# Loads of a retention block and of a gated MLP: by head over 128 partitions, k and all of w_in on GpSimd's queue

## The chip, the cores and the metric

The kernel runs on one core of a Trainium2 chip. The core has a matrix engine (TensorE, PE in the profile, with its weight loads PEld beside it), VectorE (DVE), ScalarE (ACT), GpSimd (POOL) and SyncE (SP), which here only issues transfers. Each engine works through its own instructions in order and waits for others by semaphores. Transfers between memory and the core's SBUF are issued by SP, ACT or POOL on queues of their own and are carried out by 16 DMA engines that all queues share. Matrix products land in PSUM, from where DVE or ACT copy them. The metric is the device time of one execution in microseconds, the median over the runs shown.

## The reference

q, k and v have 8 batches, 8 heads, 576 rows and 64 columns. The first part is causal attention with a decay per head and no softmax:

```python
scores = scale * np.matmul(q, k.transpose(0, 1, 3, 2))
gamma = 1.0 - 2.0 ** (-5.0 - np.arange(H, dtype=np.float32))
rel = pos[:, None] - pos[None, :]
Dmat = np.where(rel >= 0, gamma[:, None, None] ** rel[None, :, :], 0.0)
ret = scores * Dmat[None, :, :, :]
return np.matmul(ret, v).astype(np.float32)
```

Its output is laid out as 4608 tokens of 512 columns. The second part is an MLP on the tokens:

```python
h = x @ w_in                       # 512 -> 2048
sp = np.where(h > 20.0, h, np.log1p(np.exp(np.minimum(h, 20.0))))
g = h * np.tanh(sp)                # Mish
return (g @ w_out).astype(np.float32)   # 2048 -> 512
```

All inputs and the output are float32.

## The kernel before

The 576 rows of a batch are cut into chunks of 128 rows (the last 64 rows of two batches share one). Four chunks make a tile of 512 tokens; there are nine tiles. Tiles 0 and 1 hold the first chunk of each of the eight batches, which need no state from earlier rows. Later chunks add a state: the sum of k times v over the earlier rows of the batch, kept with the decay folded into q and v.

Each tile goes through attention, then `g1` (16 groups of four matmuls with w_in, each followed by Mish on ACT), then `g2` (64 matmuls with w_out) and the stores. The order of instructions on every engine is written out by hand: `manual_schedule` keeps the order of the program, so an instruction that waits holds up all that stands behind it on its engine. PE's order decides most: from tile 1 on, the steps of the next tile's attention are slipped between the groups of `g1` and `g2`.

Tiles 0 and 1 have an attention of their own, `f_...` in the code. `load_first` (L97) brings q and k of a tile with 16 loads of 128 KB on SP, each for one batch and four heads, into 32 partitions of `stage`: partition 32b+g holds four successive rows 4g to 4g+3 of batch b. `f_cast` (L176) turns a pair of heads into bf16 and sorts by the row within the four. `f_transpose` (L184) transposes 128x128 blocks (two heads by 64 columns) for each of the four rows, first q's four and then k's four, and after each four a copy brings them from PSUM to SBUF, back in the order of rows. For tile 0 q's and k's transposes have a PSUM tile each; for tile 1 they share one. `f_scores` (L199) makes the scores of a pair of heads and multiplies them on DVE with the decay mask. `f_v` (L211) casts v, `f_out` (L216) makes the output of one batch and copies it to xT; in tile 1 two batches share a PSUM tile. `f_state` (L234) scales v on POOL for the states, and `f_k` (L240) copies the cast k from SBUF to SBUF on SP into the layout that `state` (L314) reads.

v of tile 0 and the first 512 columns of w_in come on SP too (L109, L116); the latter are cast by DVE (L446). The other three quarters of w_in and all of w_out come on POOL's queue, which casts on the way; then v of tile 1 and the chunks from 8 on, three loads each (`load`, L248). After that POOL alternates between loads and the product vs (`step_v`, L271). The buffers for v (`vraw`) are five: a load waits until the product and the cast that read the buffer before are done.

Before g2 of tile 0 (`g2_first`, L385) is run in 16 steps, `first_steps` (L464) says ahead of which step a transposition or a score of tile 1 stands. `keep_warm` issues idle matmuls early on. The result buffers of `store` (L408) are three, so the fourth copy waits for the first store.

Of the kernel before, what the change touches and what calls it, by code (L numbers as in the profile page):

```python
# [10 lines left out]
F32 = mybir.dt.float32  # L11
BF16 = mybir.dt.bfloat16
AX = mybir.ActivationFunctionType
# [4 lines left out]
def kernel(  # L18
# [26 lines left out]
    KC = d_model // P  # L45
# [18 lines left out]
    first = ctx.enter_context(tc.tile_pool(name="first", bufs=1))  # L64
    io = ctx.enter_context(tc.tile_pool(name="io", bufs=PF))
# [6 lines left out]
    ps_sc = ctx.enter_context(tc.tile_pool(name="ps_sc", bufs=2, space=PS))  # L72
# [7 lines left out]
    w_in_t = wpool.tile([P, KC, d_ff], BF16)  # L80
# [1 line left out]
    w_in_r = moe_w_in.rearrange("(c p) f -> p c f", p=P)  # L82
    w_out_r = moe_w_out.rearrange("(f p) d -> p f d", p=P)

    def load_w_in(i):
        nc.gpsimd.dma_start(out=w_in_t[:, :, ts(i, 512)], in_=w_in_r[:, :, ts(i, 512)])

    def load_w_out(i):
        nc.gpsimd.dma_start(out=w_out_t[:, ts(i, 4), :], in_=w_out_r[:, ts(i, 4), :])
# [1 line left out]


    stage = gp.tile([P, 2, H, 4 * D], F32, name="gT")
    qf, kf = stage[:, 0], stage[:, 1]
    v0 = {}

    def load_first(t):  # L97
        for half in range(2):
            hs = ds(4 * half, 4)
            for dst, src in ((qf, q), (kf, k)):  # L100
                for b in range(4):
                    nc.sync.dma_start(  # L102
                        out=dst[ds(32 * b, 32), hs, :],
                        in_=src[4 * t + b, hs, 0:P, :].rearrange("h (g r) d -> g h (r d)", r=4))

    def load_first_v(t):
        for b in range(4 * t, 4 * t + 4):
            v0[b] = io.tile([P, H, D], F32, name="vraw")
            (nc.gpsimd if t else nc.sync).dma_start(out=v0[b], in_=v[b, :, 0:P, :].rearrange("h p d -> p h d"))  # L109

    load_first(0)
    load_first_v(0)
    w0 = []
    for c in range(KC):
        w0.append(io.tile([P, 512], F32, name="qraw"))
        nc.sync.dma_start(out=w0[c], in_=w_in_r[:, c, 0:512])  # L116

    zeros = consts.tile([P, 512], BF16)
    nc.vector.memset(zeros, 0.0)
    ident = consts.tile([P, P], BF16)  # L120
# [23 lines left out]
    nc.scalar.activation(gq, ex, AX.Exp)  # L144
    nc.scalar.activation(gv, ex, AX.Exp, scale=-1.0)
    warm = consts.tile([P, 1], F32)
    nc.scalar.activation(warm, pos[:, 0:1], AX.Mish)
    nc.vector.tensor_scalar(gq, gq, 1.0 / math.sqrt(D), None, op0=OP.mult)

    diag = consts.tile([P, 2], F32)  # L150
# [21 lines left out]
    k0 = {}  # L172
    v0s = {}
    fst = {}

    def f_cast(t, p, which, copy):  # L176
        if p == 0 and which == 0:
            fst[t] = {"qb": first.tile([P, 4, H, D], BF16, name="qb"),
                      "kb": first.tile([P, 4, H, D], BF16, name="kb", bufs=2), "vb": {}}
        name, src = (("qb", qf), ("kb", kf))[which]  # L180
        copy(fst[t][name][:, :, ds(2 * p, 2), :],
             src[:, ds(2 * p, 2), :].rearrange("p h (r d) -> p r h d", r=4))

    def f_transpose(t, p, copies):  # L184
        if t == 0:
            tps = [ps_h.tile([P, 4, P], BF16, name="hp") for _ in range(2)]
        else:
            both = ps_sc.tile([P, 2, 8, P], BF16, name="sc")
            tps = [both[:, i, 0:4] for i in range(2)]
        for i, name in enumerate(("qb", "kb")):  # L190
            out_t = first.tile([P, 4, P], BF16, name=name + "T", bufs=2)
            for r in range(4):
                nc.tensor.transpose(tps[i][:, r, :],
                                    fst[t][name][:, r, ds(2 * p, 2), :].rearrange("p h d -> p (h d)"), ident)
            copies[i](out_t.rearrange("p b (g r) -> p b g r", r=4),
                      tps[i].rearrange("p r (b g) -> p b g r", b=4))
            fst[t][name, p] = out_t

    def f_scores(t, p):  # L199
        qT, kT = fst[t]["qb", p], fst[t]["kb", p]  # L200
        sc = ps_sc.tile([P, 2, 4, P], F32, name="sc")
        for b in range(4):
            for e in range(2):
                r = ds(64 * e, 64)
                nc.tensor.matmul(sc[:, e, b, :], lhsT=kT[r, b, :], rhs=qT[r, b, :], start=True, stop=True)  # L205
        sm = first.tile([P, 2, 4, P], BF16, name="sm0", bufs=4)
        nc.vector.tensor_tensor(sm, sc, dmask[:, ds(2 * p, 2), :].unsqueeze(2).to_broadcast([P, 2, 4, P]),  # L207
                                op=OP.mult)
        fst[t]["sm", p] = sm

    def f_v(t, b, copy):  # L211
        vb = first.tile([P, H, D], BF16, name="vb", bufs=4)
        copy(vb, v0[4 * t + b])
        fst[t]["vb"][b] = vb

    def f_out(t, b, copy):  # L216
        if b == 0:
            xts[t] = xp.tile([P, KC, NCH * P], BF16, name="xT")
        vb = fst[t]["vb"][b]
        if t == 0:  # L220
            pool, name = ((ps_st, "st"), (ps_o, "ops"))[b % 2]
            ot = pool.tile([P, NP, P], F32, name=name)
        else:
            if b % 2 == 0:
                fst[t]["ot"] = ps_sc.tile([P, 2, NP, P], F32, name="sc")
            ot = fst[t]["ot"][:, b % 2]
        for p in range(NP):
            for e in range(2):
                nc.tensor.matmul(ot[ds(64 * e, 64), p, :], lhsT=vb[:, 2 * p + e, :],
                                 rhs=fst[t]["sm", p][:, e, b, :],  # L230
                                 start=(p == 0), stop=True, skip_group_check=True)
        copy(xts[t][:, :, ts(b, P)], ot)  # L232

    def f_state(t, b):  # L234

        n = 4 * t + b
        v0s[n] = first.tile([P, H, D], BF16, name="v0s", bufs=B)
        nc.gpsimd.tensor_tensor(v0s[n], v0[n], gv[:, 0, :].unsqueeze(2).to_broadcast([P, H, D]), op=OP.mult)

    def f_k(t, b):  # L240
        n = 4 * t + b
        k0[n] = first.tile([P, H, D], BF16, name="k0", bufs=B)
        nc.sync.dma_start(out=k0[n].rearrange("p h d -> p (h d)"),
                          in_=fst[t]["kb"][ds(32 * b, 32)].rearrange("p r h d -> p r (h d)"))

# [178 lines left out]
    dve, act, pool = nc.vector.tensor_copy, nc.scalar.copy, nc.gpsimd.tensor_copy  # L424


    for p in range(NP):
        f_cast(0, p, 0, pool if p % 2 else dve)
        f_cast(0, p, 1, pool)
    load_first(1)  # L430
    keep_warm(8)
    for p in range(NP + 1):
        if p < NP:
            f_transpose(0, p, (act, act))
            keep_warm(2)
        if p > 0:
            f_scores(0, p - 1)
    f_v(0, 0, pool)
    f_v(0, 1, act)
    f_v(0, 2, pool)  # L440
    f_v(0, 3, act)
    for i in range(1, 4):
        load_w_in(i)
    for b in range(4):
        f_out(0, b, (dve, act)[b % 2])
        dve(w_in_t[:, b, 0:512], w0[b])  # L446
    for b in range(4):
        f_state(0, b)
        f_k(0, b)
    for i in range(4):  # L450
        load_w_out(i)
    load_first_v(1)
    make_masks()


    for p in range(NP):
        f_cast(1, p, 0, dve)
        f_cast(1, p, 1, dve)
    for f in range(nF):
        g1(0, f)  # L460
    for b in range(4):
        f_k(1, b)
    load(N0)
    first_steps = {0: (f_transpose, 0), 1: (f_transpose, 1), 3: (f_scores, 0), 4: (f_scores, 1),  # L464
                   6: (f_transpose, 2), 7: (f_transpose, 3), 9: (f_scores, 2), 11: (f_scores, 3)}
    for i in range(nF):
        if i in first_steps:
            step, p = first_steps[i]
# [114 lines left out]
```

## Time and profile before

| | us |
|---|---|
| median of 3 runs | 334.22 (334.13 to 334.87) |
| the profiled execution | 335.18 |
| its span | 333.5 |
| PE busy | 309.7 (93%) |
| ACT busy | 137.6 (41%) |
| POOL busy | 136.0 (41%) |
| DVE busy | 117.2 (35%) |

The times in the profile are from the start of the span. A group's idle time is that of the engine ahead of it, with the instruction or transfer that ended it behind an arrow. In the timeline a row merges like instructions; the number of them follows the x. POOL's DMA rows are the time in which it writes a load's descriptors; when the load lands is told by another view. Matmul ends are modelled, so the last 0.2 us of a group can overlap the next. The granted clock is 1.00 at full speed and 0.50 at half.

### The profile page before, as it was taken

The page shows a single profiled execution, that of the slowest core. Times are in us where ns is not written, and L with a number is a line of the kernel's source. Part 1 is how long each engine was busy: PE and PEld are TensorE (multiplying, and loading weights), DVE is VectorE, ACT ScalarE, POOL GpSimd, SP SyncE. Part 2 cuts the span into 40 slices and gives each one's busy share as a digit, 9 for nine tenths or more (in the row PEclk, how much of TensorE's full clock was granted, in tenths as well). Part 3 has the DMA queues.
Part 4 walks back from the last instruction along what each step waited for, and adds up shares of the span by engine and source line. Part 5 has one row for each costly group of instructions (what it writes and reads, how often), then busy time and mean ns, then how long its engine had stood idle before and what let it go on. Part 6 is the DMA issues. An engine that isn't in the chain of part 4 may idle for free.

```text
span 333.5 us, 5849 instructions
## 1 busy us (share of the span) xinstructions
PE 309.7 (93%) x2400; PEld 151.5 (45%) x2400; DVE 117.2 (35%) x162; ACT 137.6 (41%) x252; POOL 136.0 (41%) x167
## 2 busy tenths in 40 slices
PE   5839788699999999999999999999999999999996
PEld 1514344335544554545445454545454544444444
DVE  2481243435533524242525152525252522000111
ACT  6526511367626653534343534334344432333300
POOL 2495325699939295444455353626310000000000
PEclk9969999879999999999999999999999999999999
DMA  7999998998889599979495959697450500010022
GB/s 176 214 268 244 241 244 153 244 170 146 156 171 165 113 128 166 148 157 191 96 191 104 184 109 176 113 173 126 82 126 15 115 31 33 31 31 33 31 79 78
DMA packets 74841, 45.46 MB, mean 136 GB/s; under 512 B 57024, under 2 KB 65984, under 8 KB 74816
## 3 DMA queue, kind: packets, MB, share of 16 engines
q0 software_dynamic: 37808, 23.08, 44.2%
q1 hardware_dynamic: 36864, 21.90, 29.8%
q8 instruction: 18, 0.29, 0.4%
q10 hardware_dynamic: 144, 0.13, 0.1%
q14 instruction: 7, 0.06, 0.1%
HBM read 36.70 MB, written 9.44 MB: 138 GB/s over the span
## 4 chain that ended last, share of the span: by engine, by line
PE 81%; DMA 9%; SPq 3%; DVE 2%; ACT 2%; issue 1%; DVEq 0%; ACTq 0%
PE hp L365 34%; PE ops L380 30%; DMA gT<-in_k_dram 6%; PE st L328 3%; PE sc L296 2%; PE hp L380 2%; PE hp L391 2%; DMA qraw<-in_moe_w_in_dram 2%; ACT ssb L332 2%; SPq L102 1%; DMA gT<-in_q_dram 1%; PE sc L346 1%; SPq L109 1%; PE hp L402 1%; PE sc L283 1%
## 5 line engine op out<-in xcount | busy, mean ns | idle before, releaser
L365 PE MATMUL hp<-xT,w_in_t 128*128 128x512 bf16 x576 | 147.6, 386 | 4.3 <-DVE xT L232 3.2
L367 ACT ACTIVATE gT<-hp 128x512 bf16<-128x512 f32 x144 | 86.1, 598 | 126.1 <-PE hp L365 124.6
L380 PE MATMUL ops<-w_out_t,gT 128*128 128x512 bf16 x464 | 117.9, 379 | 0.3 <-DVE res L410 0.3
L365 PEld LDWEIGHTS <-w_in_t 128*128 128x128 bf16 x576 | 53.8, 99 | 67.5 <-issue 4.0
L380 PEld LDWEIGHTS <-gT 128*128 128x128 bf16 x496 | 48.3, 98 | 58.4 <-issue 1.0
L410 DVE COPY res<-ops 128x512 f32<-128x512 f32 x30 | 20.7, 691 | 144.3 <-PE ops L380 143.3
L258 POOL DMA_DIRECT2D qraw<-in_q_dram x24 | 22.4, 933 | 54.0 <-DVE qks L268 52.2
L300 DVE TENSOR_TENSOR sm<-sc,mask 128x1024 bf16<-128x1024 f32 x28 | 33.0, 1216 | 10.9 <-PE sc L296 10.9
L274 POOL TENSOR_TENSOR vs<-vraw,gv 128x512 bf16<-128x512 f32 x28 | 29.7, 1074 | 12.6 <-PE sc L351 12.4
L332 ACT ACTIVATE ssb<-st,diag 128x256 bf16<-128x256 f32 x64 | 26.8, 470 | 16.9 <-PE st L328 16.9
L258 POOL DMA_DIRECT2D vraw<-in_v_dram x24 | 21.8, 908 | 6.0 <-issue 3.3
L258 POOL DMA_DIRECT2D qks<-in_k_dram x24 | 21.6, 899 | 3.0 <-DMA w_out_t<-in_moe_w_out_dram 3.0
L355 DVE CAST xT<-sc 128x512 bf16<-128x512 f32 x28 | 18.2, 686 | 11.0 <-PE sc L351 10.9
L268 DVE TENSOR_TENSOR qks<-qraw,gq 128x512 bf16<-128x512 f32 x28 | 20.5, 767 | 0.0
L207 DVE TENSOR_TENSOR sm<-sc,dmask 128x1024 bf16<-128x1024 f32 x8 | 9.7, 1222 | 9.0 <-PE sc L205 8.8
L262 POOL DMA_DIRECT2D qraw<-in_q_dram x8 | 5.6, 703 | 14.9 <-DVE qks L268 14.9
L346 PE MATMUL sc<-qkT,ssb 128*64 128x128 bf16 (+1 forms) x256 | 11.2, 215 | 0.0
L351 PE MATMUL sc<-sm,vs 128*64 128x128 bf16 x224 | 10.9, 219 | 0.0
L284 ACT COPY qkT<-sc 128x1024 bf16<-128x1024 bf16 x8 | 8.1, 1011 | 6.0 <-PE sc L283 5.9
L296 PEld LDWEIGHTS <-qkT 64*128 64x128 bf16 x224 | 6.3, 94 | 6.8 <-issue 5.9
L296 PE MATMUL sc<-qkT 64*128 64x128 bf16 x224 | 9.0, 217 | 0.0
L346 PEld LDWEIGHTS <-ssb 128*64 128x64 bf16 x256 | 7.8, 111 | 2.5 <-issue 2.5
(81 smaller groups left out, 178.7 us busy)
## 6 DMA issues: line engine op xcount, KB each, us to landing
out_dram<-res SPq DMA_DIRECT2D x31, 256.0 KB, 2.1
vraw<-in_v_dram POOLq DMA_DIRECT2D x28, 256.0 KB, 7.4
qraw<-in_q_dram POOLq DMA_DIRECT2D x24, 256.0 KB, 4.9
qks<-in_k_dram POOLq DMA_DIRECT2D x24, 128.0 KB, 6.1
gT<-in_q_dram SPq DMA_DIRECT2D x16, 128.0 KB, 4.9
gT<-in_k_dram SPq DMA_DIRECT2D x16, 128.0 KB, 6.7
w_out_t<-in_moe_w_out_dram POOLq DMA_DIRECT2D x4, 512.0 KB, 20.9
w_in_t<-in_moe_w_in_dram POOLq DMA_DIRECT2D x3, 512.0 KB, 14.1
```

The costliest lines, as they stand in the source:

```text
L258: nc.gpsimd.dma_start(out=t, in_=src[b, :, ds(P * c, P), :].rearrange("h p d -> p h d"))
L268: nc.vector.tensor_tensor(live[n]["qks"][:, 0], live[n]["q"], gq[:, c, :].unsqueeze(2).to_broadcast([P, H, D]), op=OP.mult)
L274: nc.gpsimd.tensor_tensor(vs, live[n]["v"], gv[:, c, :].unsqueeze(2).to_broadcast([P, H, D]), op=OP.mult)
L296: nc.tensor.matmul(sc[:, e, p, :], lhsT=qk[r, 1, p, :], rhs=qk[r, 0, p, :], start=True, stop=True)
L300: nc.vector.tensor_tensor(sm.rearrange("p e n i -> p (e n) i"), sc.rearrange("p e n i -> p (e n) i"), m.unsqueeze(1).to_broadcast([P, 2 * ...
L332: nc.scalar.activation(ssb[:, :, e, :], st, AX.Copy, scale=diag[:, e:e + 1])
L346: nc.tensor.matmul(ot[ds(64 * e, 64), p, ds(i0, iw)], lhsT=st_sb[bb, cc][:, p, e, :], rhs=qk[:, 0, p, ds(i0, iw)], start=(i0 == 0 and p == ...
L355: nc.vector.tensor_copy(xts[t][:, :, ts(s, P)], ot)
L365: nc.tensor.matmul(hp, lhsT=w_in_t[:, c, ts(f, P)], rhs=xts[t][:, c, :], start=(c == 0), stop=(c == KC - 1))
L367: nc.scalar.activation(gts[t][:, f, :], hp, AX.Mish)
L380: nc.tensor.matmul(ops, lhsT=gts[t][:, f, ts(s, P)], rhs=w_out_t[:, f, :], start=(f == 0), stop=(f == nF - 1))
L410: copy(ot, ops)
```

## The change

q of tiles 0 and 1 is loaded with one load per head: four batches into all 128 partitions, where partition 4g+b holds rows 4g to 4g+3 of batch b. All of q of both tiles has its place in `stage`, so tile 1's loads write another half of it. k is loaded in the same layout by POOL's queue, which casts it to bf16 directly into `kb`; the first two heads of tile 0 are issued ahead of the constants. The block of w_in that SP loaded comes on POOL's queue in two halves of 256 columns. Only q is cast by an engine, on DVE.

A transposition now takes one head's 64 columns, so there are 16 in a step instead of 8, with the two heads in the two halves of PSUM's partitions; all 16 are issued before the two copies. `f_out` of tile 1 takes a PSUM tile for each batch. The SBUF copies for the states go; k of each batch's first chunk is loaded again from memory in the states' layout, by POOL (`load_k0`), for batch 0 ahead of chunk 8's loads, for batch 1 ahead of chunk 10's, and for the others during g1 of tile 1. The load of the Mish table moves behind the scores of tile 0. w_out's first two quarters stand ahead of k of tile 1 on POOL's queue, the others behind it. Tile 1's transpositions and scores stand later in `first_steps`, and v of its batches 0 and 2 is cast by DVE.

```diff
-    def load_w_in(i):
-        nc.gpsimd.dma_start(out=w_in_t[:, :, ts(i, 512)], in_=w_in_r[:, :, ts(i, 512)])
+    def load_w_in(f0, n):
+        nc.gpsimd.dma_start(out=w_in_t[:, :, ds(f0, n)], in_=w_in_r[:, :, ds(f0, n)])
...
-    def load_first(t):
-        for half in range(2):
-            hs = ds(4 * half, 4)
-            for dst, src in ((qf, q), (kf, k)):
-                for b in range(4):
-                    nc.sync.dma_start(
-                        out=dst[ds(32 * b, 32), hs, :],
-                        in_=src[4 * t + b, hs, 0:P, :].rearrange("h (g r) d -> g h (r d)", r=4))
+    def rows(x, t, h):
+        return x[ds(4 * t, 4), h, 0:P, :].rearrange("b (g r) d -> g b (r d)", r=4)
+
+    def load_first_q(t):
+        for h in range(H):
+            nc.sync.dma_start(out=stage[:, t, h, :], in_=rows(q, t, h))
+
+    def load_first_k(t, hs):
+        if t not in kbs:
+            kbs[t] = first.tile([P, H, 4 * D], BF16, name="kb", bufs=2)
+        for h in hs:
+            nc.gpsimd.dma_start(out=kbs[t][:, h, :], in_=rows(k, t, h))
...
-    load_first(0)
+    load_first_q(0)
     load_first_v(0)
-    w0 = []
-    for c in range(KC):
-        w0.append(io.tile([P, 512], F32, name="qraw"))
-        nc.sync.dma_start(out=w0[c], in_=w_in_r[:, c, 0:512])
+    load_first_k(0, (0, 1))
...
-    nc.scalar.activation(warm, pos[:, 0:1], AX.Mish)
...
+    def f_cast(t, p, copy):
+        if p == 0:
+            fst[t] = {"qb": first.tile([P, H, 4 * D], BF16, name="qb"), "kb": kbs[t], "vb": {}}
+        copy(fst[t]["qb"][:, ds(2 * p, 2), :], stage[:, t, ds(2 * p, 2), :])
...
         for i, name in enumerate(("qb", "kb")):
+            for r in range(4):
+                for e in range(2):
+                    nc.tensor.transpose(tps[i][ds(64 * e, 64), r, :],
+                                        fst[t][name][:, 2 * p + e, ts(r, D)], ident)
+        for i, name in enumerate(("qb", "kb")):
             out_t = first.tile([P, 4, P], BF16, name=name + "T", bufs=2)
-            for r in range(4):
-                nc.tensor.transpose(tps[i][:, r, :],
-                                    fst[t][name][:, r, ds(2 * p, 2), :].rearrange("p h d -> p (h d)"), ident)
             copies[i](out_t.rearrange("p b (g r) -> p b g r", r=4),
-                      tps[i].rearrange("p r (b g) -> p b g r", b=4))
+                      tps[i].rearrange("p r (g b) -> p b g r", b=4))
...
-            if b % 2 == 0:
-                fst[t]["ot"] = ps_sc.tile([P, 2, NP, P], F32, name="sc")
-            ot = fst[t]["ot"][:, b % 2]
+            ot = ps_sc.tile([P, 2, NP, P], F32, name="sc")[:, 0]
...
-    def f_k(t, b):
-        n = 4 * t + b
-        k0[n] = first.tile([P, H, D], BF16, name="k0", bufs=B)
-        nc.sync.dma_start(out=k0[n].rearrange("p h d -> p (h d)"),
-                          in_=fst[t]["kb"][ds(32 * b, 32)].rearrange("p r h d -> p r (h d)"))
+    def load_k0(b):
+        k0[b] = first.tile([P, H, D], BF16, name="k0", bufs=B)
+        nc.gpsimd.dma_start(out=k0[b], in_=k[b, :, 0:P, :].rearrange("h p d -> p h d"))
...
+    load_first_k(0, range(2, H))
     for p in range(NP):
-        f_cast(0, p, 0, pool if p % 2 else dve)
-        f_cast(0, p, 1, pool)
-    load_first(1)
+        f_cast(0, p, dve)
     keep_warm(8)
...
+    nc.scalar.activation(warm, pos[:, 0:1], AX.Mish)
     f_v(0, 0, pool)
+    load_w_in(0, 256)
     f_v(0, 1, act)
     f_v(0, 2, pool)
+    load_w_in(256, 256)
     f_v(0, 3, act)
     for i in range(1, 4):
-        load_w_in(i)
+        load_w_in(512 * i, 512)
+    load_first_q(1)
     for b in range(4):
         f_out(0, b, (dve, act)[b % 2])
-        dve(w_in_t[:, b, 0:512], w0[b])
+    load_w_out(0)
+    load_w_out(1)
     for b in range(4):
         f_state(0, b)
-        f_k(0, b)
-    for i in range(4):
-        load_w_out(i)
+    load_first_k(1, range(H))
+    load_w_out(2)
+    load_w_out(3)
     load_first_v(1)
+    load_k0(0)
     make_masks()
...
     for p in range(NP):
-        f_cast(1, p, 0, dve)
-        f_cast(1, p, 1, dve)
+        f_cast(1, p, dve)
     for f in range(nF):
         g1(0, f)
-    for b in range(4):
-        f_k(1, b)
     load(N0)
-    first_steps = {0: (f_transpose, 0), 1: (f_transpose, 1), 3: (f_scores, 0), 4: (f_scores, 1),
-                   6: (f_transpose, 2), 7: (f_transpose, 3), 9: (f_scores, 2), 11: (f_scores, 3)}
+    first_steps = {3: (f_transpose, 0), 4: (f_transpose, 1), 6: (f_scores, 0), 7: (f_scores, 1),
+                   8: (f_transpose, 2), 9: (f_transpose, 3), 11: (f_scores, 2), 12: (f_scores, 3)}
...
     for b in range(4):
-        f_v(1, b, act if b % 2 else pool)
+        f_v(1, b, act if b % 2 else dve)
...
         f_state(1, b)
+        if b == 1:
+            load_k0(1)
         load(N0 + 1 + b)
...
         if w == 0:
+            if j < 3:
+                load_k0(2 * j + 2)
+                load_k0(2 * j + 3)
             if 0 < j:
```

More of the change, by code (lines that the diff above doesn't have):

```diff
@@ L93 @@
     stage = gp.tile([P, 2, H, 4 * D], F32, name="gT")
-    qf, kf = stage[:, 0], stage[:, 1]
+    kbs = {}
     v0 = {}
-    def load_first(t):
-        for half in range(2):
-            hs = ds(4 * half, 4)
-            for dst, src in ((qf, q), (kf, k)):
-                for b in range(4):
-                    nc.sync.dma_start(
-                        out=dst[ds(32 * b, 32), hs, :],
-                        in_=src[4 * t + b, hs, 0:P, :].rearrange("h (g r) d -> g h (r d)", r=4))
+    def rows(x, t, h):
[8 more added lines that the diff above has]
+            nc.gpsimd.dma_start(out=kbs[t][:, h, :], in_=rows(k, t, h))
     def load_first_v(t):
@@ L174 @@
     fst = {}
[L176 to L182, printed above, removed]
+    def f_cast(t, p, copy):
+        if p == 0:
+            fst[t] = {"qb": first.tile([P, H, 4 * D], BF16, name="qb"), "kb": kbs[t], "vb": {}}
+        copy(fst[t]["qb"][:, ds(2 * p, 2), :], stage[:, t, ds(2 * p, 2), :])
     def f_transpose(t, p, copies):
```

## The prediction

> **What bounds the kernel now.** I read the slices first, then busy time by stage, the chain, the waits of PE, and last the timeline and the issue-to-landing times of the loads.
>
> ```profile
> PE   5839788699999999999999999999999999999996
> PEclk9969999879999999999999999999999999999999
> ```
>
> One digit is 8.3 us. From the ninth slice on PE is full at full clock, so only the first 67 us can move the end, unless a later stage runs out of loads. By stage (time, then busy us of PE, PEld, DVE, ACT, POOL, then clock, DMA share, GB/s):
>
> ```profile
> 20.10:23.50 3.40, 0.17 (x1) 0.13 (x2) 3.40 (x4) 0.59 (x1) 3.40 (x4) 0.50 1.19 225
> 23.50:26.90 3.40, 3.40 (x10) 1.07 (x9) 0.96 (x3) 0.62 (x2) 3.40 (x6) 0.54 1.16 239
> 26.90:39.40 12.50, 12.09 (x57) 5.35 (x56) 1.68 (x5) 8.34 (x14) 4.33 (x8) 1.00 1.19 244
> 39.40:61.50 22.10, 17.93 (x129) 8.65 (x127) 10.01 (x13) 3.52 (x6) 10.36 (x12) 1.00 1.07 203
> 67.30:71.30 4.00, 4.00 (x17) 1.40 (x17) 1.71 (x2) 1.00 (x2) 3.99 (x5) 0.54 0.96 159
> 71.30:94.30 23.00, 22.76 (x232) 11.71 (x231) 10.01 (x12) 15.79 (x29) 22.92 (x27) 1.00 0.92 162
> ```
>
> PE is empty at 20.1 to 23.5, runs g1 of tile 0 at half clock to 26.6, loses 4.2 us of 22.1 in g2 of tile 0 with attention of tile 1 woven in, and starts g1 of tile 1 at 67.3, again at half clock. In the last row POOL is as full as PE: 22.92 of 23.0. The chain:
>
> ```profile
> 15.51 5.63 DMA qraw<-in_moe_w_in_dram
> 21.16 9.48 DMA gT<-in_k_dram
> 30.66 8.97 DMA gT<-in_k_dram
> ```
>
> The start is made of loads: the first block of w_in (SP), then k of tile 1 (SP). PE's waits from 39 to 68 us:
>
> ```profile
> PE sc L193 <- DVE qbT L195: 4.2, 4, 1.8
> PE sc L229 <- ACT vb L213: 2.1, 1, 2.1
> PE sc L229 <- DVE xT L232: 0.8, 1, 0.8
> PE hp L365 <- ACT xT L232: 0.7, 1, 0.7
> ```
>
> Line one: k's transposes wait for the copy of q's transposes, which sits in the other half of the same PSUM tile; line three is the same between two outputs in one tile. Last, POOL's queue:
>
> ```profile
> 16.67 2.45 POOL L86 DMA_DIRECT2D w_in_t<-in_moe_w_in_dram  x3
> 36.39 0.88 POOL L109 DMA_DIRECT2D vraw<-in_v_dram  x1 [3.25 <-DMA w_in_t<-in_moe_w_in_dram]
> 40.17 1.15 POOL L258 DMA_DIRECT2D qraw<-in_q_dram  x1 [1.76 <-DMA w_out_t<-in_moe_w_out_dram]
> 47.94 0.88 POOL L258 DMA_DIRECT2D vraw<-in_v_dram  x1 [2.70 <-DMA w_out_t<-in_moe_w_out_dram]
> ```
>
> Counting issues, each waits for the load eight places before it on that queue. Issue plus landing time gives w_in 27.7 and 35.8 (first, third), w_out 39.9 and 51.0 (first, fourth): 4.05 us each beside SP's loads, 3.7 when these thin out; the closest two blocks land at 44.1 and 47.4, and their 3.3 I take for POOL's queue alone. On SP, the casts that wait for loads (7.75, 10.17, 12.76) give 0.63 us per 128 KB alone; in tile 1 (26.63, 30.76, 35.28, 39.74) 1.1 beside POOL's.
>
> **The change part by part.**
>
> *Constants and attention of tile 0.* Two k loads go ahead of the constants on POOL. The nearest issues, 0.70 (64 partitions, 512 rows) and 0.90 (128 partitions, 1024 rows), are larger; I take 0.7, bounds 0.5 and 1.15 (the longest issue above). So ident, pos and dist, the exponentials and DVE's scaling of gq, which stands ahead of the casts, come 1.5 us later (1.0 to 2.3): first cast at 8.4, transposes 8.9 instead of 7.4. The Mish table load (1.28) and its activation (0.2) leave that place on ACT, which is free at 7.9 as before, and land after the last copy of transposes, where ACT has 1.6 us before it must copy xT: nothing; without that cover 1.5. The four k casts and two q casts on POOL (0.61 each) go; the q casts on DVE (0.43) come as their loads do.
>
> A step has 16 transposes of 64 columns instead of 8 of 128. The nearest row is 16 pairs of the same shape in step_o (L346, L351): 0.58 us of PE from 77.72 to 78.30 against 0.44 for eight full ones. I add 0.15 each at full clock, twice that at half (ends 0 and 0.45); eight steps. The last score then comes at 16.5 to 16.9 (16.14 before), the last mask product 18.9 (18.3), and f_out can run at once, where before DVE's casts of w_in (3.43 and 0.99) kept xT of b=2 until 22.59. Four products and copies of 0.6 to 0.7, two and two on DVE and ACT, end at 21.4: by the engines g1 could start there, 1.9 us earlier.
>
> *w_in wholly on POOL.* Four SP loads and four DVE casts go. Two loads of 256 columns come in, each with as many rows (512) as a 512-column one but half the bytes: 2.0 to 4.05 us of transfer beside SP, I take 3. POOL first casts v of b=0: on SP the first load lands 2.6 after the start, eight q loads take 8 x 0.63, k beside them some 2.5, v itself 1.2 (POOL's and ACT's casts of v waited that far apart): 11.4. The cast ends at 12. The first w_in of before took 11.0 us from issue to landing on a queue that fell in beside SP; less the half bytes that makes 21 to 23, I take 22, the second half 25; q of tile 1 ends on SP near 23, so the other blocks follow each 3.3: 28.3, 31.6, 34.9. g1 starts at 22 (23.3 before; 21.4 to 25), stays at half clock until 26.6, is fed block by block and ends 34.9 + 4 x 0.865 = 38.4, where it ended at 39.35.
>
> *Tile 1's q, k and w_out.* q is cast on DVE as before, long before its use. w_out 0 and 1 follow w_in on POOL's queue: 38.2, 41.5. Then eight k loads (0.5 each; ends 0.3 and 1.0, half or all of an SP load's price beside another queue). Numbers 17 to 23 of that queue each wait for the one eight before, the last of these for w_out 1; the first pair, heads 0 and 1, lands at 42.5. w_out 2 and 3 (50, 53), v, k of batch 0 and chunk 8 stand behind. The four products of f_state (4.45) on POOL hide behind the same landings. In the loop the first transposes move from step 0 to step 3: PE reaches them at 38.4 + 2.6 = 41.0 and waits 1.5 for k. That is the path: k's landing, 42.5, starts the rest.
>
> *The loop itself.* All 16 transposes are issued before either copy, so the four waits (4.2 us) go. From k's landing to the end of step 12: 10 steps of 0.865, 4 transposes of 0.65, 4 scores of 0.43, 12.95, so 55.45, where before it was 58.93. w_out 2 is wanted at 49.6, w_out 3 at 54.6: 0.4 late at worst, which I leave out.
>
> *f_out of tile 1.* Each b gets its own PSUM tile: 0.8 goes. v of b=0 and 2 is cast by DVE (0.43) instead of POOL (0.61), behind DVE's two stores: 0.4 later, under ACT's wait; behind it on DVE stands xT of b=0, which has 1 us until b=1 needs it. ACT's cast of b=1 still stands behind its copy of the fourth result, which waits for the first store to land (2.1 us of PE): stays. DVE's first store comes after the last mask product, 0.2 more. From step 12 to g1: 8.35 becomes 7.75, gain 0.6. That cast now also frees the v buffer that POOL's load of chunk 9 wants, which ran at 58.01 and now waits in front of POOL's whole queue until 58.3.
>
> *k for the state.* The eight copies from SBUF on SP go (no one waits for them); eight loads of 256 KB come on POOL, 0.90 us each to issue, like L258's k. Seven stand in the stage where POOL is full: 6.3 us. Before vs of chunk 8 stands one, before chunk 9's five, before chunk 10's seven. Counting POOL's rows (2.73 a chunk, 1.06 a product) from 58.3, vs is ready 0.9 to 1.5 us before PE wants it for each of chunks 8 to 11: nothing, but if cover is gone up to 3 us.
>
> **Skill.** The measured stretch 26.9 to 39.4 has both queues loaded: in 4.05 us one w_in (3.3 alone) and 3.7 SP loads (2.3 alone), 5.6 us of work. "DMA: Bandwidth & Descriptors", section "Rules for kernel authors", says against this change that spreading DMAs over the queues doesn't help bandwidth, since all use the same 16 engines. By that rule a mixed start of 14 us would take 4 us more, everything on POOL's queue would land that much later, and the time would be 334; the row gives the sum below.
>
> **Sum.** End of step 12: 55.45 for 58.93, -3.5. f_out: -0.6, so g1 of tile 1 starts at 63.2 for 67.28. Clock: that g1 lost half of 67.3 to 71.0, 1.9 us; I take the same (1.4 to 3.1). Together -4.1. The profiled execution took 335.18, its span 333.5; the median of three is 334.22. From the median: 330.1; its profile should show a span near 329.4.
>
> **Rivals.**
> 1. *The start is quicker.* Each load now spreads over 128 partitions instead of 32, and the two halves may land at half the price. All that POOL's queue carries lands 2 us earlier: 328.1. Against: 11 us to landing for a first load on a crowded queue.
> 2. *POOL becomes the bound of g1 of tile 1.* For: 22.92 of 23.0 and 6.3 more. If an issue of the new loads is 0.3 dearer, seven take the slack and 1 to 3 us stall: 332.0.
> 3. *Slower: one queue for everything.* Place: step 12 of the loop, which needs the last block of w_out. g1 of tile 1 starts 8.6 us after it lands (0.86 + 7.75), so the end moves back when it lands after 58.7. If v still lands at 13.7 (POOL's cast of it stands at 14.43), the first half lands 14.3 + 11.0 = 25.3; with every block at 4.05 the row is 25.3 + 2 + 5 x 4.05 + 8 x 0.55 + 2 x 4.05 = 60: g1 at 68.6, 335.5. For: all seven blocks and k in one queue. Against: SP has nothing after 23 us to share with.
> 4. *Nothing*: the first half lands at 22, but every block keeps 4.05: k's first pair comes at 22 + 3 + 5 x 4.05 + 1 = 46.3, 3.8 later than I say: 333.9.
>
> **How the numbers follow.** Forecast 0.54, own range 328.4 to 331.8; rival 1 0.15; 2 0.13; 3 0.13; 4 0.05. Faster by over 0.2% (0.67 us, about what this kernel's measurement can tell) are the first three, 0.82; same 0.05; slower 0.13. Range: from rival 1 less the slack of its clock (327.3) to beyond rival 2 (333.3).
>
> **What the profile after would show.** Right: no wait of PE's transposes on DVE's qbT after 39 us; g1 of tile 0 starting at 21 to 25 us behind w_in, ending about 38.4, and a short wait for k there; g1 of tile 1 at 62 to 64.5; POOL full until 100 us with PE not waiting for vs. Wrong: a wait for w_out or kb over 2 us in the loop (rival 3), PE waiting on vs or qks at 70 to 95 (rival 2), or no wait for k at all (rival 1).

## The result and the profile after

The changed kernel takes 330.49 us (median of 4 runs, 329.6 to 331.93), the one before 334.55 beside it (4 runs, 334.13 to 335.04). The ratio is 0.9882, with a 95% interval of 0.9843 to 0.9922. A ratio leaves out runs in which the chip was disturbed (among those of the experiments, one of 333.03 us at a granted clock of 0.95 and one of 1749.44 us), so it needn't be the quotient of the two medians. The profiled execution of the changed kernel took 329.6, its span is 327.9. Profiled executions differ by 5.6 us, medians by 4.1: single runs of both kernels scatter by about 1 us to either side.

The 40 slices of the kernel after, PE's busy tenths and the clock granted to it:

```profile
PE   4869997699999999999999999999999999999995
PEclk9979999599999999999999999999999999999999
```

PE is now full from the fourth slice to the sixth, and the third has a 6 instead of a 3. What is left of the hole is in slices seven and eight, 49 to 66 us. By stage (time, then busy us of PE, PEld, DVE, ACT, POOL, then clock, DMA share, GB/s):

```profile
20.04:23.45 3.41, 2.74 (x21) 1.43 (x19) 2.95 (x3) 0.59 (x1) 3.41 (x5) 0.50 1.22 227
23.45:36.40 12.95, 12.95 (x61) 5.70 (x60) 1.80 (x3) 8.96 (x15) 4.97 (x8) 1.00 1.26 205
36.40:54.80 18.40, 18.40 (x161) 8.30 (x159) 9.08 (x11) 3.53 (x6) 12.89 (x18) 1.00 1.15 180
54.80:62.00 7.20, 2.12 (x33) 1.68 (x33) 2.72 (x5) 2.79 (x5) 6.41 (x7) 0.69 1.26 268
62.00:66.00 4.00, 3.96 (x20) 1.56 (x20) 2.10 (x2) 1.48 (x4) 3.98 (x6) 0.70 1.47 198
66.00:88.20 22.20, 22.20 (x230) 11.40 (x229) 10.09 (x11) 15.25 (x28) 22.18 (x26) 1.00 1.29 153
```

g1 of tile 0 is no longer starved: it starts at 21.57 and ends at 36.4, 2.9 us earlier. The stage after it, g2 of tile 0 with the attention of tile 1 woven in, has PE busy for all of its 18.40 us. The stage that follows, `f_out` of tile 1, takes 7.20 us, of which PE works 2.12. POOL is full in the last row (22.18 of 22.20), and so is PE. The chain of the kernel after:

```profile
21.57 14.98 PE hp L360 x64
...
52.51 0.61 DVE res L405
53.14 5.01 DMA out_dram<-res
58.25 0.59 ACT res L405
58.84 0.53 ACT vb L212
59.41 0.66 PE sc L226 x8
...
62.03 3.04 PE hp L360 x8
```

No load stands in it from 21.57 on: what stands between g2 of tile 0 and g1 of tile 1 is a store. DVE's copy of the first result ends at 53.1, the store lands 5.0 us later, and only then has ACT a buffer for the fourth result; its cast of v stands behind that copy, and PE behind the cast. PE's waits between 20 and 140 us:

```profile
PE sc L226 <- ACT vb L212: 3.9, 1, 3.9
PE hp L360 <- ACT xT L229: 1.3, 2, 0.7
PE st L226 <- DVE xT L229: 0.6, 1, 0.6
```

The 4.2 us behind the copies of transposes are gone; the wait for ACT's cast has grown from 2.1 to 3.9. Last, the timeline of some instructions, and the landing times of the stores issued from 50 to 66 us:

```profile
8.75 1.10 DVE L179 CAST qb<-gT 128x512 bf16<-128x512 f32 x3
...
28.80 0.54 POOL L108 DMA_DIRECT2D kb<-in_k_dram  x1 [1.97 <-DMA w_in_t<-in_moe_w_in_dram]
31.38 0.53 POOL L108 DMA_DIRECT2D kb<-in_k_dram  x1 [2.05 <-DMA w_in_t<-in_moe_w_in_dram]
33.90 0.53 POOL L108 DMA_DIRECT2D kb<-in_k_dram  x1 [1.99 <-DMA w_out_t<-in_moe_w_out_dram]
36.42 0.53 POOL L108 DMA_DIRECT2D kb<-in_k_dram  x1 [1.99 <-DMA w_out_t<-in_moe_w_out_dram]
...
55.56 0.89 POOL L253 DMA_DIRECT2D vraw<-in_v_dram  x1 [4.19 <-DVE vb L212]
...
58.25 0.59 ACT L405 COPY res<-st 128x512 f32<-128x512 f32 x1 [4.55 <-DMA out_dram<-res]
```

```profile
DMA to landing us min/median/max: 3.9/4.9/5.1
```

Four k issues each wait for the load eight places before them, and so show when the blocks of w_in and w_out land: one each 2.5 us. Before, the first store took 3.0 us to land (the smallest of its stage, 3.0/4.3/4.9).

### The profile page after: what moved, and what is told of

It reads as the page before. It is cut to its first block, busy times and chain, and to the rows that moved or that the text cites. A ratio compares the mean times of both kernels' runs of the same rounds, so it can differ in the third digit from the quotient of the medians.

```text
span 327.9 us, 5939 instructions
## 1 busy us (share of the span) xinstructions
PE 308.8 (94%) x2464; PEld 150.9 (46%) x2464; DVE 115.5 (35%) x158; ACT 137.3 (42%) x252; POOL 148.1 (45%) x185
## 4 chain that ended last, share of the span: by engine, by line
PE 89%; ACT 4%; DVE 3%; DMA 2%; issue 1%; POOL 1%; ACTq 0%; DVEq 0%; POOLq 0%
PE hp L360 39%; PE ops L375 31%; PE st L323 3%; PE sc L291 2%; PE hp L375 2%; PE hp L386 2%; ACT ssb L327 2%; DMA out_dram<-res 2%; PE sc L341 1%; DVE sm L206 1%; PE hp L397 1%; PE sc L278 1%; PE hp L190 1%; PE sc L346 1%; PE ops L168 1%
## 5 line engine op out<-in xcount | busy, mean ns | idle before, releaser
L253 POOL DMA_DIRECT2D qks<-in_k_dram x24 | 21.6, 901 | 0.0
L108 POOL DMA_DIRECT2D kb<-in_k_dram x16 | 9.1, 584 | 8.8 <-DMA w_in_t<-in_moe_w_in_dram 4.0
```

The lines of the kernel that those rows point to most:

```text
L253: nc.gpsimd.dma_start(out=t, in_=src[b, :, ds(P * c, P), :].rearrange("h p d -> p h d"))
```

## The experiments

The question is where a gain of 4 us comes from. My theory was the prediction's: waits behind copies removed, less what k's landing gives back. The rivals: the loads carry the gain; or either part would do, since something behind them sets the end. The kernel before had medians of 334.64, 334.12, 335.57 and 335.67 beside the four groups of runs.

**The order alone, and the loads alone.** The first puts the new order and the separate PSUM tiles into the kernel before, with its loads, layouts and transposes of 128 columns as they were:

```diff
         for i, name in enumerate(("qb", "kb")):
-            out_t = first.tile([P, 4, P], BF16, name=name + "T", bufs=2)
             for r in range(4):
...
+        for i, name in enumerate(("qb", "kb")):
+            out_t = first.tile([P, 4, P], BF16, name=name + "T", bufs=2)
             copies[i](out_t.rearrange("p b (g r) -> p b g r", r=4),
...
-            if b % 2 == 0:
-                fst[t]["ot"] = ps_sc.tile([P, 2, NP, P], F32, name="sc")
-            ot = fst[t]["ot"][:, b % 2]
+            ot = ps_sc.tile([P, 2, NP, P], F32, name="sc")[:, 0]
```

> The kernel before with only the order of PSUM work changed: both transposes of a step ahead of both copies, and an own PSUM tile for each batch in f_out of tile 1; all loads as before. Theory (the order carries the gain): the four waits on qbT (4.2 us) and the 0.8 in f_out go, less about 1 because k of tile 1 lands only at 39.6 us: 331, no wait of the transposes on DVE left. Rival (the loads carry it): the loop waits for k and w_out anyway, 333.9 to 334.5.

The second takes these same two things out of the changed kernel:

```diff
-        for i, name in enumerate(("qb", "kb")):
             out_t = first.tile([P, 4, P], BF16, name=name + "T", bufs=2)
...
-            ot = ps_sc.tile([P, 2, NP, P], F32, name="sc")[:, 0]
+            if b % 2 == 0:
+                fst[t]["ot"] = ps_sc.tile([P, 2, NP, P], F32, name="sc")
+            ot = fst[t]["ot"][:, b % 2]
```

> The changed kernel with the old order of PSUM work: k's transposes behind the copy of q's, and one PSUM tile for two batches in f_out of tile 1. Theory (order): 3 to 4.5 us come back, 333.5 to 335, with PE waiting on qbT again. Rival (loads): 330.5 to 331.5.

Order alone: 329.7 us, ratio 0.9854 [0.9803, 0.9905], which is all that the whole change brings. Loads alone: 332.4, ratio 0.9957 [0.9921, 0.9992]. Both together are the changed kernel, 0.9882: the two gains, 1.5% and 0.4%, come to more than its 1.2%. By the intervals alone that difference isn't clear of the noise; the stages show where it goes. Which of the first run's two edits carries how much was not tried; the waits that they remove are 4.2 us (four behind the copies of transposes) and 0.8 (one in `f_out`). PE's waits and two stages of the kernel with the order alone (the stages in the columns used above):

```profile
PE sc L228 <- ACT vb L214: 2.0, 1, 2.0
PE hp L364 <- DVE xT L231: 1.2, 1, 1.2
```

```profile
56.63:61.15 4.52, 1.40 (x33) 1.11 (x33) 2.19 (x3) 2.78 (x5) 4.51 (x5) 1.00 1.12 244
61.15:65.00 3.85, 3.85 (x17) 1.35 (x17) 1.84 (x2) 1.20 (x3) 3.84 (x5) 0.56 1.36 266
```

The waits for qbT are gone here too. Its chain shows the end of g1, a step of transposes and the group behind it:

```profile
23.26 16.03 PE hp L364 x64
39.29 0.45 PE sc L192 x8
39.73 0.86 PE hp L390 x4
```

With the old loads g1 of tile 0 ends at 39.29 by the chain, 2.7 us later than in the changed kernel (21.57 + 14.98 = 36.55), and yet g1 of tile 1 starts earlier, 61.15 for 62.03. The 2.7 and 0.9 more are won back in two places. From the end of g1 to the end of g2 it takes 17.3 us for 18.25: a step of eight transposes takes 0.45 and the next group 0.86, where sixteen of 64 columns take 0.57 and the next group 0.97, so 0.23 four times over, 0.9 us. And `f_out` takes 4.5 for 7.2, 2.7 us less: ACT's cast is awaited for 2.0 instead of 3.9, and at full clock PE's part is 1.4 instead of 2.1.

PE's waits in the kernel with the loads alone:

```profile
PE sc L190 <- DVE qbT L193: 3.3, 4, 0.9
PE hp L361 <- ACT xT L230: 1.3, 2, 0.7
PE sc L227 <- ACT vb L211: 1.1, 1, 1.1
```

The waits behind the copies of transposes are back, 3.3 of the 4.2, but the wait for ACT has fallen from 3.9 to 1.1, since the store now lands in 2.2 us (median). So the time came out about 1 us below what I had expected of it: as long as the stores decide, an earlier PE is partly paid back.

**Chunk 9's v first.** In the changed kernel, POOL's load of chunk 9's v waits for a cast. Here it stands ahead of q and k of that chunk, so that POOL's queue issues nothing while the first store is under way:

```diff
+        parts = ((qr, q), (qks[:, 1], k), (vr, v))
-        for t, src in ((qr, q), (qks[:, 1], k), (vr, v)):
+        for t, src in (parts[2:] + parts[:2] if v_first else parts):
...
-        load(N0 + 1 + b)
+        load(N0 + 1 + b, b == 0)
```

> The changed kernel with chunk 9's load of v ahead of its q and k, so that POOL stands still at v and the first store of tile 0 meets fewer loads. Theory (loads that share the DMA engines made the store land after 5.0 instead of 3.0 us): it lands after 3 to 4 us, the wait in f_out shrinks by 1 to 2; POOL is 1.8 us later at vs of chunk 8, which may give up to 1.5 back: 329 to 330. Rival (the store's landing has nothing to do with those loads): still 5.0 us, 330.5 or slower.

332.81, ratio 0.9933 [0.9899, 0.9967], slower than the changed kernel where I had expected 329 to 330. The landing times of the stores and PE's waits:

```profile
DMA to landing us min/median/max: 2.1/2.2/2.3
```

```profile
PE sc L347 <- POOL vs L270: 3.5, 1, 3.5
PE hp L361 <- ACT xT L229: 1.3, 2, 0.7
PE sc L226 <- ACT vb L212: 1.1, 1, 1.1
```

The first half of the theory holds: without POOL's loads beside it a store lands in 2.2 us instead of 4.9, ACT's cast is awaited for 1.1, and g1 of tile 1 starts at 59.77. The second half doesn't. All of POOL's next loads now stand behind that v, and its first product vs, that of chunk 8, stands behind them:

```profile
72.77 1.07 POOL L270 TENSOR_TENSOR vs<-vraw,gv 128x512 bf16<-128x512 f32 x1
```

In the changed kernel this product starts at 68.41. PE waits 3.5 us for it from 70.4, and the clock is halved again from 73.1 to 79.9.

**Four result buffers.** The wait for the store can be had away without touching the loads:

```diff
-        ot = op.tile([P, d_model], F32, name="res")
+        ot = op.tile([P, d_model], F32, name="res", bufs=4)
```

> The changed kernel with four result buffers instead of three, so that the fourth copy on ACT does not wait for the first store. Theory (the 3.9 us wait in f_out of tile 1 is that store's landing, which the loads made 5.0 us long): PE's wait on ACT's cast falls below 1 us and the time by 2.5 to 4: 326.5 to 328. Rival (POOL's loads are the next bound right behind it): PE waits for vs or qks instead, gain under 1.5: 329 or more.

327.7, ratio 0.9818 [0.9754, 0.9882]. PE's waits:

```profile
PE sc L346 <- POOL vs L269: 0.7, 1, 0.7
...
PE sc L226 <- ACT vb L212: 0.5, 1, 0.5
```

The store still takes 4.8 us to land, but nobody waits. g1 of tile 1 starts at 58.24, 3.8 us earlier than in the changed kernel; the time falls by 2.8 only, and PE now waits for POOL's vs.

**The same buffer with the old loads.** The order alone, and this edit on top of it:

```diff
-        ot = op.tile([P, d_model], F32, name="res")
+        ot = op.tile([P, d_model], F32, name="res", bufs=4)
```

> The kernel before with the new order of PSUM work and four result buffers; the old loads and the SBUF copies of k stay. Theory (the order and the fourth copy's wait are what counts, the new loads are worth nothing at the end): the 2.0 us wait of the order alone falls below 0.6 and the time to 327.5 to 329, within 1 us of the changed kernel with four buffers (327.7). Rival (with that wait gone, the quicker start of the new loads comes through): 1.5 to 3 us slower than that, 329.2 to 330.7.

328.37, ratio 0.9812 [0.9773, 0.985]. That is within the interval of the run with the new loads. g1 of tile 1 starts at 59.33, 1.1 later; a wait of 0.8 for ACT's cast remains, and two behind it:

```profile
PE sc L295 <- DMA qkT<-qks: 1.7, 1, 1.7
PE sc L350 <- POOL vs L273: 1.3, 1, 1.3
```

The first of these, near 136 us, is for a transposition by DMA; the order alone has it with 0.5, and why it is longer here was not tried. The second says that POOL is late with and without the new loads of k.

**One load of k for the state.** Four result buffers, and only batch 0's k is loaded for the states, which the other batches use as well, so seven of the eight loads that the change adds are left out:

```diff
     def load_k0(b):
+        if b > 0:
+            k0[b] = k0[0]
+            return
```

> The changed kernel with four result buffers and only the first of the eight k loads for the state; the states of batches 1 to 7 are made with batch 0's k, so the output is not the reference's. Theory (POOL's issue of those loads is hidden up to the 0.7 us wait for vs that four buffers showed): that wait goes, 326.5 to 327.7. Rival (the seven loads cost their 6.3 us of POOL further on): 325 or less.

327.21, ratio 0.9771 [0.9724, 0.9817], against 327.7 with all eight: no difference that this tells. PE's wait for vs is even 1.4 us instead of 0.7. The 0.9 us that each of the loads takes POOL cost nothing at the end that these runs can tell, and the wait for vs isn't theirs.

**The casts of v earlier.** What both keep is the late start of POOL's loads from chunk 9 on, which wait for the casts of tile 1's v. Here these stand in the loop, two ahead of step 10 and two ahead of step 13, with four result buffers and the new loads:

```diff
+        if i in (10, 13):
+            for b in ((0, 1), (2, 3))[i // 13]:
+                f_v(1, b, act if b % 2 else dve)
         g2_first(i // 4, i % 4)
     for b in range(4):
-        f_v(1, b, act if b % 2 else dve)
-    for b in range(4):
         f_out(1, b, (dve, act)[b % 2])
```

> The changed kernel with four result buffers and tile 1's casts of v moved into the loop (batches 0 and 1 ahead of step 10, 2 and 3 ahead of step 13), so that POOL's load of chunk 9 no longer waits for a cast behind DVE's stores. Theory (POOL held by that cast, 4.7 us, is what makes vs late): POOL runs 4 us earlier, no wait for vs, f_out starts without waiting for ACT, 326 to 327.5. Rival (the freed POOL brings more loads into the same stretch and the loop's own loads suffer): 328 or more.

325.31, ratio 0.9718 [0.9676, 0.9759]. PE's waits, and the stage of `f_out`:

```profile
PE hp L360 <- ACT xT L229: 1.3, 2, 0.7
PE sc L278 <- DVE qks L263: 0.9, 1, 0.9
PE sc L226 <- DVE xT L229: 0.6, 1, 0.6
```

```profile
57.00:62.00 5.00, 3.75 (x41) 2.18 (x42) 3.11 (x4) 3.01 (x7) 4.99 (x7) 1.00 1.42 293
```

```profile
56.23 0.64 PE L226 MATMUL sc<-sm,vb 128*64 128x128 bf16 x16
...
58.74 1.02 PE L360 MATMUL hp<-xT,w_in_t 128*128 128x512 bf16 x4 [0.67 <-ACT xT L229]
```

The wait for vs is gone. In `f_out` PE rests only 0.56 and 0.67 us at a time, g1 of tile 1 starts at 58.74, and the clock stays at 1.00 from 26.64 to 323.6 us. In this execution g1 of tile 0 still ran at half clock until 26.64, where the changed kernel had full clock back at 23.45, so it ended some 1.5 us later.

**The same with three buffers.** To see whether the casts alone would do, the result buffers stay at three, and only the casts move:

```diff
+        if i in (10, 13):
+            for b in ((0, 1), (2, 3))[i // 13]:
+                f_v(1, b, act if b % 2 else dve)
         g2_first(i // 4, i % 4)
     for b in range(4):
-        f_v(1, b, act if b % 2 else dve)
-    for b in range(4):
         f_out(1, b, (dve, act)[b % 2])
```

> The changed kernel with v of tile 1 cast in the loop but the three result buffers kept. Theory (ACT's fourth copy still waits for the first store and xT of b=1 stands behind it): the wait of PE moves from the cast of v to xT, g1 of tile 1 starts at most 1 us earlier than 62.0, 329.3 to 330.7. Rival (the wait was the cast's own place in the order): PE's wait falls below 1 us, 327 or less.

329.73, ratio 0.9836 [0.9785, 0.9886]. The longest of PE's waits:

```profile
PE sc L226 <- ACT xT L229: 4.5, 1, 4.5
```

The cast no longer waits, but ACT's copy to xT stands behind the same copy of the fourth result: the wait for the store stays and has another name.

**The old loads with both.** The order, four buffers and the early casts on top of the kernel before, without any of the new loads, layouts or transposes:

```diff
+        if i in (10, 13):
+            for b in ((0, 1), (2, 3))[i // 13]:
+                f_v(1, b, act if b % 2 else dve)
         g2_first(i // 4, i % 4)
     for b in range(4):
-        f_v(1, b, act if b % 2 else pool)
-    for b in range(4):
         f_out(1, b, (dve, act)[b % 2])
```

> The kernel before, old loads and SBUF copies of k, with the new order of PSUM work, four result buffers and v of tile 1 cast in the loop by ACT and DVE. Theory (the new loads are worth their quicker start of 1.5 to 3 us as soon as nothing behind them waits): 327 to 328.5, clearly slower than the changed kernel with the same two edits (325.3). Rival (the new loads are worth nothing at all): 325 to 326.2.

325.5, ratio 0.9708 [0.9662, 0.9755]: the same as with the new loads, where I had expected the new ones to be worth 1.5 to 3 us. The stages (same columns):

```profile
39.00:57.00 18.00, 17.79 (x144) 8.98 (x145) 11.08 (x12) 5.04 (x10) 8.66 (x10) 1.00 1.23 227
57.00:62.00 5.00, 3.71 (x43) 1.95 (x39) 3.88 (x4) 3.01 (x7) 4.99 (x6) 1.00 1.24 291
```

```profile
56.57 0.64 PE L228 MATMUL sc<-sm,vb 128*64 128x128 bf16 x16
...
59.08 1.24 PE L364 MATMUL hp<-xT,w_in_t 128*128 128x512 bf16 x4 [0.67 <-ACT xT L231]
```

g1 of tile 0 begins at 23.33 for 21.59 with the new loads, `f_out` of tile 1 at 56.57 for 56.23, g1 of tile 1 at 59.08 for 58.74. Of the 1.7 us that the new loads are ahead at the first place, 0.3 are left at the other two. Some 0.5 went in g1 of tile 0, which stood 1.0 us longer at half clock in this execution, and 0.9 in the loop, where each of the four steps of sixteen transposes costs 0.23 more with the group behind it, as above. The new layout thus takes back half of what its loads win. The rest of the execution is 264.4 us for 265.5, with the wait of 0.9 for qks in the latter alone.

**No k ahead of the constants.** The changed kernel delays its start with two k loads ahead of the constants on POOL. Without that:

```diff
-    load_first_k(0, (0, 1))
...
-    load_first_k(0, range(2, H))
+    load_first_k(0, range(H))
```

> The changed kernel with no k load ahead of the constants on POOL. Theory (the constants delayed the first cast by the 1.8 us between 6.93 and 8.75, but what the start wins is lost at the wait for the first store): first cast near 7, g1 of tile 0 starts up to 1 us earlier, the wait in f_out of tile 1 grows by as much, 330 to 331. Rival (the start counts in full): 1 us or more faster, 329 or less.

330.72, ratio 0.9877 [0.9837, 0.9918], the same as the changed kernel. PE's first wait and the stores' landing times:

```profile
PE sc L225 <- ACT vb L211: 5.8, 1, 5.8
```

```profile
DMA to landing us min/median/max: 4.6/7.1/7.6
```

The first cast comes at 7.01 instead of 8.75, g1 of tile 0 at 19.24 instead of 21.57. g1 runs into the landings of w_in (a wait of 1.2) and ends at 35.7, only 0.7 us earlier, and so does the loop (54.1 for 54.8). The first store, issued 0.7 us earlier, lands 1.2 us later, and g1 of tile 1 starts at 63.17, 1.1 us later than in the changed kernel.

The same on top of the new loads with early casts and four buffers:

```diff
-    load_first_k(0, (0, 1))
...
-    load_first_k(0, range(2, H))
+    load_first_k(0, range(H))
```

> The changed kernel with four result buffers, v of tile 1 cast in the loop, and no k load ahead of the constants. Theory (the start counts once the wait for the store is gone): g1 of tile 0 starts near 19.3 instead of 21.6 and ends 0.7 to 1.7 us earlier, and so does the kernel, 323.5 to 324.7 where the same without the early start took 325.3. Rival (another wait takes it, most likely POOL's): 325 to 326.

Three runs took 324.94, 325.93 and 326.07, against 325.31 with the k loads first (ratio to the kernel before 0.9699 [0.9653, 0.9744]). The fourth, of 333.03, is the profiled one, so its stages aren't compared. Here too an earlier start buys nothing that can be measured.

**k of the states later.** Last, the wait for qks that the best new-load version has at 88.9 us. Six of the eight k loads are moved to much later groups of the same stage's loop:

```diff
-            if j < 3:
-                load_k0(2 * j + 2)
-                load_k0(2 * j + 3)
+            for b in {4: (2, 3), 5: (4, 5, 6, 7)}.get(j, ()):
+                load_k0(b)
```

> The changed kernel with four result buffers, v of tile 1 cast in the loop, and the k loads of batches 2 to 7 for the state moved from groups 0, 4 and 8 of g1 of tile 1 to groups 16 and 20, behind POOL's first loads and products. Theory (what the new loads still win at the start, 0.6 us at g1 of tile 1 against the old loads with the same edits, is lost again to a wait of 0.9 us for qks at 89 us, behind POOL's late loads): that wait goes, 324.2 to 325. Rival (the wait comes from elsewhere): 325.3 as without the move, or slower.

325.43 (median of five runs, 324.32 to 326.66; a sixth took 1749.44), ratio 0.9707 [0.9669, 0.9744]. PE's wait for qks is still 0.9 us, at 88.4. So the place of POOL's k loads isn't its cause. In the version without the move, DVE copies a result from 87.67, and only from 88.28 makes the two products for qks (2.07 us) that PE wants at 88.9; that this copy ahead of them is the cause was not tried.

Nine of the executions side by side, in us. All have the new order of transposes but the first and third:

| | g1 of tile 0 starts | g1 of tile 1 starts | half clock after that | span |
|---|---|---|---|---|
| before | 23.3 | 67.3 | 3.7 | 333.5 |
| after | 21.6 | 62.0 | 2.4 | 327.9 |
| loads alone | 21.4 | 64.4 | 2.9 | 330.6 |
| order alone | 23.3 | 61.2 | 3.4 | 327.8 |
| order, four buffers | 23.3 | 59.3 | 0 | 327.1 |
| after, four buffers | 21.6 | 58.2 | 3.1 | 325.4 |
| after, four buffers, casts early | 21.6 | 58.7 | 0 | 324.2 |
| order, four buffers, casts early | 23.3 | 59.1 | 0 | 323.5 |
| after, constants first | 19.2 | 63.2 | 3.1 | 329.3 |

The second column decides, with half of the third added; the first hardly matters. What the span holds beyond these two is 264.4 to 264.9 us in six of the nine. It is 265.5 and 265.7 in the two versions of the changed kernel with four buffers, where PE waits 0.9 for qks or 0.7 for vs, and 267.8 with the order and four buffers, where it waits 1.3 for vs and 1.7 for the transposition by DMA. The two versions with four buffers and early casts beat both kernels, by about 2.8% against the one before, and the simpler of them has none of the new loads.

## Why the prediction was right, step by step

The time (330.1 for 330.49) and the mechanism of the largest gain, the waits behind copies that go, were right. But the path that it named, from k's landing, was not the one that came, several terms were mis-sized, and that the time came out within 0.4 us is partly luck: the two largest errors cancel, and what is left of them is covered by the scatter of the runs.

*Constants and attention of tile 0.* Right. The first cast came at 8.75 (8.4 said), the first transposes at 9.23 (8.9), the two k issues took 1.31 us together, from a start 0.5 us later than I had it. g1 of tile 0 began at 21.57 (22 said), but behind ACT's copy to xT and not behind w_in, whose first half had landed at 19.2. A step of transposes costs 0.12 us more and makes the next group 0.11 dearer, 0.23 for the 0.15 that I took.

*w_in on POOL, "the other blocks follow each 3.3".* This term failed on size. The halves landed at 19.2 and 22.6 (22 and 25 said), and after the last q of tile 1 had landed, at 25.1, POOL's queue alone needed 2.5 us for a block. The two blocks of before from which I took 3.3 (landed at 44.1 and 47.4) were therefore not the price of a queue alone; SP issued four copies of k from 40.87 on beside them. All that stands behind w_in came earlier than I had it: k's first pair at 36.9 for 42.5. So the wait of 1.5 us for k, on which I let the whole of the loop hang, didn't occur, and the end of step 12 was 52.0 instead of 55.45. My sign of rival 1, no wait for k at all, is what came, but not its time of 328.1: the runs with the constants first and with the old loads show that what is won at the start is not there at the end.

The rule weighed there, from the Trainium skill ("DMA: Bandwidth & Descriptors", "Rules for kernel authors"), would have made 334 by the prediction's working; from its own row, 5.6 us of work in 4.05, a mixed stretch of 14 us would become 19.4, so 5.4 more and not 4. Its landings are refuted by the 36.9 for k. With 2.5 us for a block alone, the work in that row is 4.8 us and not 5.6, so most of what I took there for a gain of mixing came from the 3.3. That the changed loads bring no time is what the pair 325.31 and 325.5 shows, for other reasons than bandwidth: their lead of 1.7 us is used up by the half clock, the dearer transposes and a later wait.

*The loop itself.* Right: no wait for qbT is left, PE is busy for 18.40 of 18.40 us, and from the first transposes (39.07) to the end of step 12 it takes 13.0 us (12.95 said). The run with the order alone shows that this and the separate PSUM tiles carry a gain as large as the whole change's.

*`f_out` of tile 1, "8.35 becomes 7.75".* Failed, by 2.2 us: it took 10.0 from the end of step 12. I let the wait for the first store stay at 2.1, as if a store took 3.0 us to land whatever ran beside it. It took 5.0, among POOL's loads of chunks 8 and 9, and 2.2 where chunk 9's were held back. This error hid the one before it: 3.4 earlier at step 12, 2.2 later here.

*k for the state.* Right, and by more than I knew: POOL is full (22.18 of 22.2), PE doesn't wait for vs, and with four buffers seven fewer loads change nothing that can be measured. Rival 2 didn't occur, but it was near. With four buffers, where g1 of tile 1 starts at 58 to 59 us instead of 62, PE waits for vs, 0.7 to 1.4 us, and the cause I gave, the new loads' issue time, is not it: the wait goes with the casts of v that free the buffers for POOL's loads.

*Clock.* The half clock cost g1 of tile 1 1.2 us for the 1.9 that I took. *Sum.* g1 of tile 1 starts 5.25 us earlier (-4.1 said), and the clock gives 0.7 more, near the 5.6 between the two spans. That the medians are only 4.1 apart is because the profiled execution of before was 0.6 above its median and that of after 0.9 below.

Rivals 3 and 4 are refuted by the landings: the last block of w_out was there at 47.1, not 60, and k's first pair at 36.9, not 46.3.

## What to carry to other kernels

Where two outputs share a PSUM tile, read the waits of PE for "the other half": giving each its own tile, or issuing both before either copy, was worth here as much as a rewrite of all first loads. Before paying for an earlier start, follow what stands between it and the end in program order: an engine's copy that waits for a store to free its buffer gives an early start back, and a fourth buffer is cheaper than the loads. Add up too what the layout that the loads need costs behind them: here four times 0.23 us of transposes for a lead of 1.7. When a change has two parts, run each alone; here the parts gained 1.5% and 0.4%, 1.2% together, and their stages showed that one gain was bought off by a wait further on.

## What the runs showed of the hardware

- A store of 256 KB took 2.2 us to land where POOL's queue issued no loads beside it, 4.9 among these loads in the changed kernel, and 7.1 in the run with the constants first, where it was issued 0.7 us earlier (medians of one stage). That these loads are what holds it up was tried once, by holding them back; why 4.9 became 7.1 was not.
- Blocks of 512 KB in bf16, cast on the way by POOL's queue, landed 2.5 us apart with SP's queue idle, and 4.05 apart with SP's loads beside them in the kernel before.
- The granted clock changes in steps of 3.41 us: stretches at half speed lasted 3.41 or 6.83, but for the last, which the end cuts off. In the stage of `f_out` the two kernels with four buffers that differ only in k's loads for the states had the same gaps on PE (0.52, 0.41 and 0.67 us): one was halved from 57.91 to 61.33, the other not at all. So, by an estimate, one such step, half of 3.41 or 1.7 us, can be the clock's and not the kernel's between two runs of like kernels.
- Sixteen transposes of 64 columns took 0.57 us against 0.45 for eight of 128, and the group of matmuls after them 0.97 against 0.86.
